# A scheduler's account of the port that GpSimd and VectorE share, GpSimd's traced durations, and a settings string found anew, in a kernel of two attention and two FFN layers

## The chip, the cores and the metric

The kernel runs on one core of a Trainium2 chip. A core has five engines, each with an instruction stream of its own: TensorE (PE in the profile; PEld is its weight load), ScalarE (ACT), VectorE (DVE), GpSimd (POOL) and SyncE (SP), which here issues the DMAs. The metric is the device time of one launch in microseconds (us), as the median of several runs.

## The reference

`x` has 2048 rows of 512, all in bf16. Attention A and FFN B are applied twice with the same weights, each behind a layer normalization and added to `x`:

```python
def _A_ref(x, wqkv, wo):            # D = 512, H = 32 heads of Dh = 16
    qkv = (x @ wqkv).reshape(B, S, 3, H, Dh).transpose(2, 0, 3, 1, 4)
    q, k, v = qkv[0], qkv[1], qkv[2]
    p = _softmax(jnp.einsum("bhqd,bhkd->bhqk", q, k) * Dh ** -0.5)
    o = jnp.einsum("bhqk,bhkd->bhqd", p, v)
    return o.transpose(0, 2, 1, 3).reshape(B, S, D) @ wo
def _B_ref(x, w1, b1, w2, b2):      # F = 1376
    h = _gelu(jnp.einsum("bsd,df->bsf", _layernorm(x), w1) + b1)
    return jnp.einsum("bsf,fd->bsd", h, w2) + b2
x = A_x
x = x + _A_ref(_layernorm(x), A_wqkv, A_wo)
x = x + _B_ref(_layernorm(x), B_w1, B_b1, B_w2, B_b2)
x = x + _A_ref(_layernorm(x), A_wqkv, A_wo)
x = x + _B_ref(_layernorm(x), B_w1, B_b1, B_w2, B_b2)
```

The heavy part is the softmax: 32 heads x 2048 x 2048 scores in each of two layers, 268 million exponentials in all.

## The kernel before, in words

**Layers and segments.** The four steps are called layers 0 to 3 in the code: `L` is 1 for the first attention and FFN, 3 for the second. Heads go in eight groups of four (`hg`), queries in units of 512 (`units`, `qc`); the last unit of layer 3 is cut into 256, 128 and 128 queries. One unit and one head group make a segment. The first unit of either layer is cut over the keys too: part 0 takes the key tiles that are ready early, part 1 the others, and the two are merged with running sums. In layer 1, part 0 is the first 4 of the 16 key tiles and part 1 the other 12; in layer 3 it is 12 and 4. All eight head groups go through part 0 before part 1 begins (`build_segments`).

**One score tile.** A tile is 128 keys by 512 queries of one head. PE computes it into one PSUM bank (L1536, four heads beside each other in the array). Then one of two engines takes the exponential. ACT does it for groups of two or three banks at once (L1521, output `PT`). DVE does it for one bank at a time: L1628 reads the bank and writes the scores, scaled beforehand, as 16-bit integers, whose bits are those of an approximate bf16 exponential; shift copies then add constants to these bits (L1659 of 1024 elements, then L1667 of 2048), so that four terms stand for one tile. Two batches that are due together are joined to one copy (L1614 and L1615, twice the size). The code calls these D tiles. PE multiplies the results into the accumulator (L1741: `PT` and `dp` against `V` for plain values, and against `vs`, scaled copies of V, for the shifted terms). When a segment is through, `job_segend` transposes the accumulator on DVE (L1771), merges the parts on POOL (L1784, L1792 to L1795), divides (L1797, L1801, L1807) and passes it to the output projection (L1821).

**What must come before a part's scores.** The scores carry a bound on each query's largest score, made from norms of q and k. When a part begins, `job_scl` works out the bound on the keys: a maximum `nm` on DVE (L1223), its transpose on PE (L1225), a maximum on DVE, a square root on POOL (L1228, a power), a product on DVE (`krhs`), a small matmul on PE (L1231), and `scl` on DVE (L1232). Only then can `job_qt` write the scaled queries `QT` (L1262; on DVE for five segments, on POOL for the others), and only then can the part's scores go out. Other work of POOL: `vs` (L1287), the normalizations' application in layers' middles (`ln_apply`, L951), their reciprocal roots (`ln_group`, the power in L942), bounds on the queries (L1095 to L1099), squares (L1057), a memset (L859).

**What sets the order.** `Sched` simulates the five engines in Python and writes out every engine's instructions in the order in which its simulation issued them; on the chip each engine follows its list, and semaphores hold an instruction until what it reads is there. Each task has a priority and instructions with planned durations in microseconds. `best` picks for an engine the task of lowest priority number among those whose inputs are ready (`task_ready`, L382); scores have 0.0, products with V 1.0, D tiles' shift copies 0.15 to 2.5, `job_scl` and `job_qt` some 0.3 to 0.5. `post_prio` (L1828) gives the priority of what follows a unit's attention: 0.95 for the last two units of layer 1 and those of layer 3 from `LATE3` on, else 2.2. Of that, the FFN's additions of the bias (L1911) run at it minus 0.7, and the normalization and the projections q, k and v of the next layer (L1016, `job_lnqkv`) at it minus 0.8. `d_solo` and `take_d` give a tile to DVE when its planned work is short.

**The settings string.** `Hint.ORDER` has one base-36 digit for every four groups of exponentials (`STEP`). A digit picks one of 12 `MODES`: each changes one threshold of the scheduler, as how short DVE's work must be to give it a tile (`D_IDLE`), how full a turn of products must be (`PV_LEAST`), how late scores may be before other PE work is held (`HOLD_LATE`). So the string reshuffles the whole order without changing what is computed.

**The port.** The plan knows that a POOL instruction slows DVE's fast copies. `self.hits` (L79) keeps POOL's last four instructions with their planned times and a penalty (`lat` of a POOL instruction, 0.09 to 0.38). A DVE instruction marked "fast" (the shift copies and some others) that overlaps one in the plan is lengthened by that penalty; POOL is never delayed by DVE in the plan (L141 to L144).

**Fillers and tail.** Behind the schedule, `refill` lays the plan once more and puts matmuls on zeros (`zw`, L1425, L1427, L1429) into PE's gaps, sized in the plan. `job_tail` orders the end: the last exponentials, a table load for Gelu (L1998), Gelu on ACT (L1934, L1935) over what the FFN's first matrix product (L1882) and the additions L1911 have left for the unit ahead (in `h`), its second product (L1943), transposes behind the last normalization (L2053), and the last unit's own FFN (L1882, L2004).

## Time and profile before

| | us |
|---|---|
| median of 3 runs | 1540.3 (1538.06, 1540.3, 1541.64) |
| span of the profiled execution | 1535.9 |
| profiled execution's own time around that span | not shown |
| ACT busy | 1502.5 |
| PE busy, fillers included | 1486.8 |
| DVE busy | 1442.2 |
| POOL busy | 343.0 |
| PE's zero matmuls, L1429, L1427 and L1425 | 147.1, 119.5 and 87.4 |

A row of the profile names a line, engine, operation and its tiles, then the count, the busy time and the mean of one in ns, and last the idle time of the engine just ahead of these instructions with what ended most of it. A timeline's row begins with the start and the duration in us; neighbouring instructions of one form are drawn together (x10), and square brackets at the end hold the idle time before. A row of the chain that ended last has the start, the time that it adds, engine, tile and line. PE's matmuls overlap, so that its share isn't a utilization; idle time of an engine that isn't the bound costs nothing.

### The profile page before, as it was taken

The page shows a single profiled execution, that of the slowest core. Times are in us where ns is not written, and L with a number is a line of the kernel's source. Part 1 is how long each engine was busy: PE and PEld are TensorE (multiplying, and loading weights), DVE is VectorE, ACT ScalarE, POOL GpSimd, SP SyncE. Part 2 cuts the span into 40 slices and gives each one's busy share as a digit, 9 for nine tenths or more (in the row PEclk, how much of TensorE's full clock was granted, in tenths as well). Part 3 has the DMA queues.
Part 4 walks back from the last instruction along what each step waited for, and adds up shares of the span by engine and source line. Part 5 has one row for each costly group of instructions (what it writes and reads, how often), then busy time and mean ns, then how long its engine had stood idle before and what let it go on. Part 6 is the DMA issues. An engine that isn't in the chain of part 4 may idle for free.

```text
span 1535.9 us, 41170 instructions
## 1 busy us (share of the span) xinstructions
PE 1486.8 (97%) x17654; PEld 491.3 (32%) x17654; DVE 1442.2 (94%) x2661; ACT 1502.5 (98%) x1346; POOL 343.0 (22%) x570
## 2 busy tenths in 40 slices
PE   9999999999999999999999999999999999999998
PEld 3222222222222222222322332222222222344555
DVE  8799999999999999999999899999999989998786
ACT  8999999999999999999999999999999999999897
POOL 3576321102120022202322138220002000020110
PEclk9999999999999999999999999999999999999999
DMA  6663102213312123214842332210011001120221
GB/s 163 120 154 91 32 22 34 51 35 68 82 48 63 37 64 84 56 35 100 138 69 64 60 87 63 53 30 18 22 36 35 14 27 32 36 49 18 73 67 30
DMA packets 212487, 90.55 MB, mean 59 GB/s; under 512 B 182251, under 2 KB 207184, under 8 KB 212304
## 3 DMA queue, kind: packets, MB, share of 16 engines
q1 hardware_dynamic: 212304, 87.92, 25.6%
q8 instruction: 138, 2.26, 0.6%
q14 instruction: 45, 0.37, 0.1%
HBM read 36.81 MB, written 19.48 MB: 37 GB/s over the span
## 4 chain that ended last, share of the span: by engine, by line
ACT 44%; PE 27%; DVE 24%; issue 3%; POOL 2%; DMA 0%; DVEq 0%; POOLq 0%
ACT PT L1521 41%; DVE dp L1628 10%; PE ps L1536 9%; PE ps L1741 8%; PE ps L1943 3%; DVE dp L1667 3%; PE ps L1882 2%; PE ps L1016 2%; ACT h L1934 2%; DVE dp L1615 2%; DVE dp L1659 1%; PE ps L1425 1%; DVE accT L1771 1%; DVE st L933 1%; DVE dp L1614 1%
## 5 line engine op out<-in xcount | busy, mean ns | idle before, releaser
L1521 ACT ACTIVATE PT<-ps 128x1536 bf16<-128x1536 f32 (+1 forms) x1256 | 1422.0, 1309 | 20.6 <-PE ps L1536 18.8
L1628 DVE TENSOR_SCALAR dp<-ps 128x512 uint16<-128x512 f32 x979 | 648.8, 679 | 33.7 <-PE ps L1536 30.4
L1536 PE MATMUL ps<-QT,KT 32*128 32x512 bf16 (+2 forms) x5120 | 602.6, 340 | 23.9 <-ACT PT L1521 7.5
L1741 PE MATMUL ps<-PT,V 128*17 128x512 bf16 (+2 forms) x3899 | 491.1, 338 | 0.6 <-issue 0.5
L1741 PE MATMUL ps<-dp,vs 128*17 128x512 bf16 (+2 forms) x3663 | 460.8, 339 | 2.7 <-issue 1.8
L1536 PEld LDWEIGHTS ps<-QT,KT 32*128 32x128 bf16 x5120 | 174.1, 91 | 543.6 <-ACT PT L1521 297.6
L1262 POOL TENSOR_SCALAR QT<-qraw,scl,qbias 128x512 bf16<-128x512 bf16 (+2 forms) x91 | 75.2, 827 | 762.8 <-PE ps L1536 754.3
L1741 PE MATMUL ps<-dp,V 128*17 128x512 bf16 (+2 forms) x1221 | 232.3, 340 | 1.6 <-DVE accT L1771 1.2
L1667 DVE TENSOR_SCALAR dp<-dp 128x2048 uint16<-128x2048 uint16 x310 | 214.3, 694 | 4.9 <-PE ps L1741 1.8
L1741 PEld LDWEIGHTS ps<-dp,vs 128*17 128x17 bf16 x3663 | 124.1, 89 | 114.1 <-issue 84.8
L1741 PEld LDWEIGHTS ps<-PT,V 128*17 128x17 bf16 x3899 | 126.9, 89 | 94.2 <-issue 75.1
L1429 PE MATMUL ps<-zw 128*32 128x448 bf16 (+23 forms) x1514 | 147.1, 322 | 0.1
L1659 DVE TENSOR_SCALAR dp<-dp 128x1024 uint16<-128x1024 uint16 (+1 forms) x298 | 126.1, 426 | 2.6
L1427 PE MATMUL ps<-zw 32*128 32x444 bf16 (+7 forms) x386 | 119.5, 332 | 0.0
L1615 DVE TENSOR_SCALAR dp<-dp 128x4096 uint16<-128x4096 uint16 x91 | 111.0, 1225 | 0.6 <-PE ps L1741 0.4
L1882 PE MATMUL ps<-yT,wf 128*128 128x512 bf16 (+5 forms) x440 | 102.7, 340 | 2.1 <-issue 1.0
L1016 PE MATMUL ps<-wqkv,xnT 128*128 128x512 bf16 x336 | 91.7, 382 | 4.1 <-DVE h L1029 1.1
L1425 PE MATMUL ps<-zw 128*128 128x448 bf16 (+14 forms) x347 | 87.4, 338 | 4.4 <-DVE onec L809 2.1
L1287 POOL TENSOR_SCALAR vs<-V 128x340 bf16<-128x340 bf16 (+2 forms) x72 | 64.3, 894 | 23.0 <-PE ps L1741 16.2
L1741 PEld LDWEIGHTS ps<-dp,V 128*17 128x17 bf16 x1221 | 58.2, 89 | 34.6 <-issue 19.4
L1614 DVE TENSOR_SCALAR dp<-dp 128x2048 uint16<-128x2048 uint16 x97 | 67.8, 700 | 0.0
L1771 DVE STREAM_TRANSPOSE accT<-ps 128x512 f32<-128x512 f32 (+2 forms) x96 | 59.2, 617 | 5.3 <-PE ps L1741 5.0
(201 smaller groups left out, 1053.4 us busy)
## 6 DMA issues: line engine op xcount, KB each, us to landing
vs<-vs_scr SPq DMA_DIRECT2D x64, 255.0 KB, 2.8
wf<-in_B_w_dram SPq DMA_DIRECT2D x90, 128.0 KB, 2.5
q_scr<-qk SPq DMA_DIRECT2D x20, 256.0 KB, 2.0
k_scr<-qk SPq DMA_DIRECT2D x12, 256.0 KB, 2.1
out_dram<-xres SPq DMA_DIRECT2D x16, 128.0 KB, 1.7
vs_scr<-vs SPq DMA_DIRECT2D x8, 255.0 KB, 3.3
xres<-in_A_x_dram SPq DMA_DIRECT2D x7, 256.0 KB, 5.3
v_scr<-vst SPq DMA_DIRECT2D x12, 136.0 KB, 1.7
```

Of the source, the lines that this page charges most:

```text
L1016: yield Task("pe", prio if c0 == 0 else min(prio, HINT.LIN2), [I(lambda e, c=c: e.matmul(self.ps[:, b, :], lhsT=xnT[:, c, :], rhs=self.wqk ...
L1425: fn = lambda e: e.matmul(self.ps[:, b, 0:w], lhsT=self.zw[:, 0:128], rhs=self.zw[:, 0:w], start=st, stop=st, skip_group_check=True)
L1427: fn = lambda e: e.matmul(self.ps[:, b, 0:w], lhsT=self.zw[32 * p:32 * p + 32, 0:128], rhs=self.zw[32 * p:32 * p + 32, 0:w], start=st, sto ...
L1429: fn = lambda e: e.matmul(self.ps[32 * p:32 * p + 32, b, 0:w], lhsT=self.zw[:, 0:32], rhs=self.zw[:, 0:w], start=st, stop=st, skip_group_c ...
L1521: S_.submit(Task("act", 1e-5 * gi, [I(lambda e, pt=pt, n=n, b0=b0: e.activation(out=self.PT[:, pt:pt + n, :], in_=self.ps[:, b0:b0 + n, :] ...
L1536: return [I(lambda e, kb=kb, i=i: e.matmul(self.ps[:, b, i * W:(i + 1) * W], lhsT=self.KT[32 * hp:32 * hp + 32, hg, kb * 128:(kb + 1) * 12 ...
L1615: return lambda e: e.tensor_scalar(out=self.both(x[1], y[1]), in0=self.both(x[0], y[0]), scalar1=float(SHIFT[2]), scalar2=None, op0=ALU.add)
L1628: self.S_.submit(Task("dve", 0.0, [I(lambda e: e.tensor_scalar(out=self.dpu(u)[:, w * 512:(w + 1) * 512], in0=self.ps[:, b, :], scalar1=BI ...
L1659: t = Task("dve", prio(), [I(lambda e: e.tensor_scalar(out=self.dpu(u + 1)[:, 0:N], in0=self.dpu(u)[:, 0:N], scalar1=float(SHIFT[1]), scal ...
L1667: t = Task("dve", prio(), [I(lambda e: e.tensor_scalar(out=self.dpp(v)[:, :, 0:N], in0=self.dpp(u)[:, :, 0:N], scalar1=float(SHIFT[2]), sc ...
L1741: ops.append((nth[j, sh] + 0.1 * i, I(lambda e, hp=hp, v=v, ap=ap[:, i * W:(i + 1) * W], first=first and i == 0, W=W: e.matmul(self.ps[32 ...
L1882: yield Task("pe", self.soft(pr if c0 == 0 else min(pr, HINT.LIN2)) if y0 == 0 else pr, [I(lambda e, c=c: e.matmul(self.ps[0:M, b, 0:W], l ...
```

## The change

The account of the port is written anew. Two fields hold until when DVE's last fast copy and POOL's last instruction hold the port. In the plan a POOL instruction now starts its body (behind a head of 0.2 us) only when DVE's fast copy is through, and a fast copy starts its body (behind 0.137 us) only when a POOL body that began before it is through. POOL instructions marked "brief" wait but don't hold the port. `task_ready` counts the port as an input of fast instructions. POOL's planned durations are set to those of traces, the penalties go, and more instructions of DVE carry the mark "fast". `post_prio` is 0.7 for layer 1's last unit. `ORDER` is another string. Lines of the changed kernel stand 20 higher than before: L1225 is L1245 there, L1536 is L1556, and so on.

```diff
+POOL_HEAD = 0.2
+DVE_HEAD = 0.137
...
-        self.hits = []
+        self.dve_port = (0.0, None)
+        self.pool_port = (0.0, 0.0)
...
             if eng == "pool":
-                self.hits = self.hits[-3:] + [(op.t0, op.t0 + dur, lat or 0.0)]
+                if lat == "after" and self.dve_port[1] is not None:
+                    order = self.dve_port[1]
+                    op.t0 = max(op.t0, order.t1 + LATENCY["pool"])
+                body = max(op.t0 + POOL_HEAD, self.dve_port[0])
+                dur = body + max(0.0, dur - POOL_HEAD) - op.t0
+                if lat != "brief":
+                    self.pool_port = (body, op.t0 + dur)
                 lat = None
             elif lat == "fast":
-                dur += sum(h for t0, t1, h in self.hits if t0 < op.t0 + dur and op.t0 < t1)
+                body = op.t0 + DVE_HEAD
+                if self.pool_port[0] <= body:
+                    body = max(body, self.pool_port[1])
+                dur = body + dur - DVE_HEAD - op.t0
+                self.dve_port = (op.t0 + dur, op)
                 lat = None
...
+            if lat == "fast":
+                r = max(r, P.pool_port[1] - DVE_HEAD)
+            elif lat == "after":
+                r = max(r, P.dve_port[0] + LATENCY["pool"])
         return r
...
-    ORDER = '617843148821304205503107024723209000040207043042340397211914350542770442973009430070000450240024504940493349800001430000505010133104559a211a2540320233040
+    ORDER = '570045030800534070003002303031403011030303420031020034192500022b801b50250500300400000803023509000452700079002734800534200030954433a3559a70034a55a507024090
...
     def ln_apply(self, tt, slot, i, dst, dres, prio, eng="dve"):
...
-                                         [("x", tt), ("nmr", slot), ("rs", slot)], [dres], 0.92, (), 0.09)])
+                                         [("x", tt), ("nmr", slot), ("rs", slot)], [dres], 0.77)])
...
     def job_qt(self, sg, s):
...
-0.16 + 0.24 * W / 512 if eng == "dve" else 0.43 + 0.52 * W / 512, (), "fast" if eng == "dve" else 0.09)])
+0.16 + 0.24 * W / 512 if eng == "dve" else 0.34 + 0.43 * W / 512, (), "fast" if eng == "dve" else None)])
...
     def post_prio(self, L, qc):
-        return 0.95 if L == 1 and qc >= self.NC - 2 or L == 3 and qc >= LATE3 else 2.2
+        return 0.7 if L == 1 and qc == self.NC - 1 else 0.95 if L == 1 and qc >= self.NC - 2 or L == 3 and qc >= LATE3 else 2.2
```

The durations not shown: `vs` 0.27 + 0.17 for each key tile to 0.21 + 0.17; the segment's merges 0.70 to 0.62 and 0.75 to 0.73; the powers 0.45 to 0.42 (plus 0.153 a column) and, in `job_scl`, 0.55 to 0.60, both "brief"; the bounds' small products 0.26 to 0.38 before, 0.22 to 0.33 now, "brief".

The change moves instructions in nearly every row of the order. Three places follow. The first is PE where layer 3 goes from part 0 to part 1, as it was: L1225 transposes `nm`, L1231 multiplies `krhs`, L1536 are scores, L1741 products with V.

```order
L1536 MATMUL ps<-QT,KT 128x512 x3
L1427 MATMUL ps<-zw 128x444
L1741 MATMUL ps<-PT,V 17x512
L1741 MATMUL ps<-dp,vs 17x512
L1741 MATMUL ps<-PT,V 17x512 x2
L1741 MATMUL ps<-dp,vs 17x512 x3
L1429 MATMUL ps<-zw 32x444
L1429 MATMUL ps<-zw 32x366 x4
L1225 MATMUL ps<-ident,nm 32x128
L1741 MATMUL ps<-dp,vs 17x512
L1741 MATMUL ps<-PT,V 17x512 x3
L1741 MATMUL ps<-dp,V 17x512
```

And as it is now:

```order
L1245 MATMUL ps<-ident,nm 32x128
L1556 MATMUL ps<-QT,KT 128x512 x2
L1447 MATMUL ps<-zw 128x444
L1556 MATMUL ps<-QT,KT 128x512
L1447 MATMUL ps<-zw 128x444
L1761 MATMUL ps<-PT,V 17x512
L1761 MATMUL ps<-dp,vs 17x512
L1761 MATMUL ps<-PT,V 17x512 x3
...
L1761 MATMUL ps<-dp,vs 17x512 x2
L1556 MATMUL ps<-QT,KT 128x512 x2
L1251 MATMUL ps<-krhs,sel 128x8
```

Before, the last scores of part 0 stand ahead of L1225, and the next scores come 14 rows behind L1231; now five tiles of scores stand between L1245 and L1251. The second place is PE where layer 1 goes from part 0 to part 1, as it was:

```order
L1225 MATMUL ps<-ident,nm 32x128
L1536 MATMUL ps<-QT,KT 128x512 x2
L1427 MATMUL ps<-zw 128x444
L1741 MATMUL ps<-PT,V 17x512 x4
L1429 MATMUL ps<-zw 32x448 x8
L1429 MATMUL ps<-zw 32x226 x4
L1536 MATMUL ps<-QT,KT 128x512 x3
L1741 MATMUL ps<-PT,V 17x512 x3
L1429 MATMUL ps<-zw 32x444
L1429 MATMUL ps<-zw 32x200 x4
L1231 MATMUL ps<-krhs,sel 128x8
```

And as it is now:

```order
L1556 MATMUL ps<-QT,KT 128x512 x3
L1761 MATMUL ps<-PT,V 17x512 x3
L1449 MATMUL ps<-zw 32x444
...
L1245 MATMUL ps<-ident,nm 32x128
L1761 MATMUL ps<-PT,V 17x512
...
L1251 MATMUL ps<-krhs,sel 128x8
L1445 MATMUL ps<-zw 128x448 x3
L1445 MATMUL ps<-zw 128x398
L1556 MATMUL ps<-QT,KT 128x512
```

Before, five tiles of scores stand between the two small matmuls; now the last scores of part 0 stand ahead of both, with products and fillers behind them. The third place is DVE's end: L1771 transposes the accumulator, L1797 and L1801 divide, L1803 transposes the result for the projection, L1911 adds the FFN's bias. As it was:

```order
L1659 TENSOR_SCALAR dp<-dp 128x1024
L1667 TENSOR_SCALAR dp<-dp 128x2048
L1911 TENSOR_SCALAR h<-ps,b1c 96x128
L1771 STREAM_TRANSPOSE accT<-ps 128x128
L1797 RECIPROCAL rv<-accT 128x4
L1801 TENSOR_TENSOR obl<-accT,rv 128x4x16
L1803 STREAM_TRANSPOSE dp<-obl 128x128
```

And as it is now:

```order
L1823 STREAM_TRANSPOSE dp<-obl 128x128
L1931 TENSOR_SCALAR h<-ps,b1c 128x128
L1791 STREAM_TRANSPOSE accT<-ps 128x128
L1931 TENSOR_SCALAR h<-ps,b1c 128x128
L1817 RECIPROCAL rv<-accT 128x4
L1931 TENSOR_SCALAR h<-ps,b1c 128x128
L1821 TENSOR_TENSOR obl<-accT,rv 128x4x16
L1931 TENSOR_SCALAR h<-ps,b1c 128x128 x4
L1823 STREAM_TRANSPOSE dp<-obl 128x128
L1931 TENSOR_SCALAR h<-ps,b1c 96x128
```

Before, the last addition L1911 stands ahead of the last two heads' ends; now eight additions stand behind the last but one L1823 (which was L1803).

55 lines of the change are left out of this document (29 added, 26 removed).

## The prediction

> **What bounds the kernel now.** I read the page first, then the groups by shape, the waits, the timeline at the longest waits, and the chain that ended last.
>
> The page, its first row and the group of the attention exponentials:
>
> ```profile
> PE 1486.8 (97%) x17654; PEld 491.3 (32%) x17654; DVE 1442.2 (94%) x2661; ACT 1502.5 (98%) x1346; POOL 343.0 (22%) x570
> L1521 ACT ACTIVATE PT<-ps 128x1536 bf16<-128x1536 f32 (+1 forms) x1256 | 1422.0, 1309 | 20.6 <-PE ps L1536 18.8
> ```
>
> ScalarE (ACT) is busy 98% of 1535.9 us, and VectorE (DVE) 94%. PE's 97% holds filler matmuls on zeros and says little. ACT stands still for 33.4 us in all, 20.6 of them ahead of its exponentials. GpSimd (POOL) is busy for 22%: a change in its timing acts only through DVE, which meets it at a port, or through a chain that POOL is a link of. So the kernel's time is ACT's work, plus ACT's waits, plus a short start and tail. I count the change in those terms.
>
> The group of exponentials by shape:
>
> ```profile
> L1521 ACT ACTIVATE PT<-ps 128x1536 bf16<-128x1536 f32 x605 | 924.6, 1528 | 14.6 <-PE ps L1536 13.2
> L1521 ACT ACTIVATE PT<-ps 128x1024 bf16<-128x1024 f32 x651 | 712.5, 1105 | 5.9 <-PE ps L1536 5.7
> ```
>
> One more bank of 512 columns costs 1528 - 1105 = 423 ns. The 605 x 3 + 651 x 2 = 3117 banks take 1318.5 us of the 1422.0, and the remaining 103.5 us over 1256 instructions is 82 ns for each instruction.
>
> DVE's part of the softmax, by shape:
>
> ```profile
> L1628 DVE TENSOR_SCALAR dp<-ps 128x512 uint16<-128x512 f32 x979 | 648.8, 679 | 33.7 <-PE ps L1536 30.4
> L1667 DVE TENSOR_SCALAR dp<-dp 128x2048 uint16<-128x2048 uint16 x305 | 212.2, 699 | 4.9 <-PE ps L1741 1.8
> L1659 DVE TENSOR_SCALAR dp<-dp 128x1024 uint16<-128x1024 uint16 x293 | 124.7, 429 | 2.6
> L1615 DVE TENSOR_SCALAR dp<-dp 128x4096 uint16<-128x4096 uint16 x91 | 111.0, 1225 | 0.6 <-PE ps L1741 0.4
> L1614 DVE TENSOR_SCALAR dp<-dp 128x2048 uint16<-128x2048 uint16 x97 | 67.8, 700 | 0.0
> ```
>
> The last four are the shift copies, which meet POOL. What a meeting costs shows in the timelines of POOL and of DVE around 1432 us:
>
> ```profile
> 1432.14 1.53 POOL L859 MEMSET dp<- 128x512 bf16 x2 [7.69 <-PE ps L1741]
> 1433.13 0.82 DVE L1659 TENSOR_SCALAR dp<-dp 128x1024 uint16<-128x1024 uint16 x1
> 1437.06 0.42 DVE L1659 TENSOR_SCALAR dp<-dp 128x1024 uint16<-128x1024 uint16 x1
> 1437.52 0.69 DVE L1667 TENSOR_SCALAR dp<-dp 128x2048 uint16<-128x2048 uint16 x1
> ```
>
> Beside POOL's memsets the copy of 1024 takes 0.82 us, alone 0.42. On the mean the port costs little: against an undisturbed 0.42 and 0.68 (the 0.69 above is its display to 10 ns), 293 x 0.009 + 305 x 0.019 + 97 x 0.020 = 10.4 us of DVE time in the three largest groups. That is the stock from which a better account of the port can draw; it's not on ACT's clock until DVE is late with a bank or a P tile.
>
> **The change, part by part.** *The account alone* runs nowhere on the chip. It and the new ORDER string decide which instruction stands where; the sum is over the places where that shows.
>
> *Work moved between ACT and DVE.* Counting rows, ACT issues 604 exponentials of three banks and 655 of two: 3122 banks in 1259 instructions, 5 and 3 more. That is 5 x 0.423 + 3 x 0.082 = **+2.4 us** on the engine that bounds. DVE gets 974 loads for 979 (-3.4 us), 9 fewer joined copies at L1614 (-6.3) and 6 fewer at L1615 (-7.4), against 21 more single copies at L1659 and 15 more at L1667, 11 of each short: at 0.28 and 0.42 apiece (what the page's totals, next, leave for the five short ones of before) that is +7.4 and +7.4. DVE is 2.3 us lighter, which doesn't lie on the path: ACT doesn't wait for DVE's sum.
>
> ```profile
> L1667 DVE TENSOR_SCALAR dp<-dp 128x2048 uint16<-128x2048 uint16 x310 | 214.3, 694 | 4.9 <-PE ps L1741 1.8
> L1659 DVE TENSOR_SCALAR dp<-dp 128x1024 uint16<-128x1024 uint16 (+1 forms) x298 | 126.1, 426 | 2.6
> ```
>
> *The change of part in layer 3.* ACT's longest wait of the steady state and the chain behind it (timelines of ACT, PE, POOL):
>
> ```profile
> 920.45 11.40 ACT L1521 ACTIVATE PT<-ps 128x1024 bf16<-128x1024 f32 x10 [2.47 <-PE ps L1536]
> 915.78 0.39 PE L1536 MATMUL ps<-QT,KT 32*128 32x512 bf16 x3
> 916.84 0.23 PE L1225 MATMUL ps<-ident,nm 128*32 128x128 bf16 x1
> 918.58 0.17 PE L1231 MATMUL ps<-krhs,sel 32*128 32x8 bf16 x1
> 919.20 1.52 POOL L1262 TENSOR_SCALAR QT<-qraw,scl,qbias 128x512 bf16<-128x512 bf16 x2 [0.22 <-DVE scl L1232]
> 920.02 0.39 PE L1536 MATMUL ps<-QT,KT 32*128 32x512 bf16 x4
> ```
>
> The last scores of part 0 go out at 915.78, ACT is through with them at 917.98, and the first scores of part 1 need the key bound (L1225, L1231) and QT: 3.18 us from L1225 to them. In the changed order five score tiles stand behind the transpose of the bound, two of them just ahead of L1231's successor; ACT gets 5 x 0.423 + 2 x 0.082 = 2.3 us more to do inside the chain. The 2.47 us shrink to some 0.2: **-2.3 us**. Bounds: -2.47 if all goes, 0 if the chain itself gets later by as much, since its start hangs on the last tiles of layer 1.
>
> *The change of part in layer 1* goes the other way. Before (chain that ended last, and ACT's timeline):
>
> ```profile
> 75.92 1.40 PE ps L1016 x6
> 82.33 0.17 PE ps L1231
> 83.50 0.44 PE ps L1536 x3
> 83.93 7.80 ACT L1521 ACTIVATE PT<-ps 128x1024 bf16<-128x1024 f32 x7 [0.27 <-PE ps L1536]
> ```
>
> Here the chain costs ACT 0.27 us, since 13 score tiles stand behind the last projections (L1016), 5 of them behind L1225. In the new order all 128 tiles of part 0 stand ahead of the transpose and nothing between it and the first scores of part 1: the picture of 916 us above, with QT on DVE, which isn't slower. There ACT waited 2.47, so here it should wait about 2.2 more than its 0.27, unless the start is quicker: ACT also waits elsewhere in its first 60 us, the longest for 1.37 us:
>
> ```profile
> 36.64 20.73 ACT L1521 ACTIVATE PT<-ps 128x1536 bf16<-128x1536 f32 x18 [1.37 <-PE ps L1536]
> ```
>
> What is saved there is lost in the wait behind it, and the net is the arrival of the chain. I take **+1.5 us**, between -0.3 (all of the 0.27 gone) and +3.3 (the whole 3.18 chain bare and its last link).
>
> *The tail.* The chain that ended last, and four rows of DVE:
>
> ```profile
> 1521.25 1.28 ACT L1998
> 1522.74 1.17 ACT h L1934
> 1524.30 2.33 PE ps L1943 x10
> 1526.63 0.24 PE ps L2053 x4
> 1516.97 0.34 DVE L1911 TENSOR_SCALAR h<-ps,b1c 128x128 bf16<-128x128 f32 x1
> 1517.23 0.41 DVE L1659 TENSOR_SCALAR dp<-dp 128x1024 uint16<-128x1024 uint16 x1
> 1518.29 0.34 DVE L1911 TENSOR_SCALAR h<-ps,b1c 96x128 bf16<-96x128 f32 x1
> 1522.55 0.31 DVE L1803 STREAM_TRANSPOSE dp<-obl 128x128 bf16<-128x128 bf16 x1
> ```
>
> Before, the last FFN1 result of the unit ahead (L1911) is out at 1518.6, so that Gelu starts as soon as its table is in. In the new order 28 of its matmuls stand behind the last PV, and eight of its additions behind the last transpose but one (L1803), six of them between the last L1771 and the last L1803. At 0.26 us from start to start (1517.23 - 1516.97) five hold the transpose back by 1.3 us (the sixth falls into the gaps between dependent instructions), and Gelu, behind the eighth, starts near 1524.5 and not at 1522.7. Two of the ten L1943 now stand behind L2053, which gives back 2 x 0.23. **+1.3 us**, between 0 and +1.9. The cover that hid this work before were the last exponentials.
>
> *The port.* ACT's 18.8 us behind scores were 48 waits. Without the 2.47, 1.37 and the 2.13 below, 12.8 us are left in 45 waits of 0.28 us: this is jitter, of which the lock may be one cause. If the planner now lays other work under a held port, a part goes. Upper bound of the gain: 10.4 us of DVE, if each were ACT's; lower: nothing, or a loss of the same kind as the scatter moves, which I set at 2. I take a quarter of the 12.8: **-3.2 us**. For what POOL holds, the row:
>
> ```profile
> 699.10 1.04 POOL L942 TENSOR_TENSOR rs<-rs,cneg 128x4 f32<-128x4 f32 x1
> 699.22 0.68 DVE L1614 TENSOR_SCALAR dp<-dp 128x2048 uint16<-128x2048 uint16 x1
> ```
>
> The copy that begins inside the power runs in its undisturbed 0.68 us, as the new mark "brief" has it. The Trainium skill, in "SBUF — State Buffer", section "Who interferes with whom", says that whichever engine issues first has the shared pair for the whole instruction and the other fully blocks. By that the copy would have ended only after 1.04 - 0.12 + 0.68 us, and the new marks would leave out waits of up to 0.9 us at each of the 19 powers, 17 us of DVE at most; the trace doesn't agree for these small operands, and the sum goes by the row.
>
> *The stall at 1437 us.*
>
> ```profile
> 1439.20 0.22 PE L1741 MATMUL ps<-dp,vs 128*17 128x128 bf16 x1 [1.84 <-issue]
> 1439.91 2.37 ACT L1521 ACTIVATE PT<-ps 128x1536 bf16<-128x1536 f32 x2 [2.13 <-PE ps L1536]
> ```
>
> PE stands for 1.84 us behind nothing that the profile shows, in the stage of narrow tiles, and ACT pays 2.13. No rule of the scheduler knows of it. It may go or come again elsewhere: 0, between -2.1 and +2.1.
>
> **Sum:** 2.4 - 2.3 + 1.5 + 1.3 - 3.2 + 0 = -0.3 us on the profiled 1535.9. What lies around the span isn't shown for that execution; the median of the runs, 1540.3, stands 4.4 above it, and I keep that: **1540.0 us, no change**. Its own range, with the unknown terms each some way to their bounds, is 1537 to 1543. A measurement can tell 0.2% here, 3.1 us, since the runs shown lie 3.6 apart.
>
> **The rivals.**
>
> *The port was the cause of most small waits.* Then the account takes out two thirds of the 12.8 us, and the stall at 1437, which follows the memsets that held DVE, goes with them: -0.3 - 5.3 - 2.1 gives 1532.6. For it: the 0.82 against 0.42, and that POOL's late copies stand in both long chains. Against it: only 10.4 us of DVE, and five tiles less for DVE in the new order, which doesn't look like an engine with time to spare.
>
> *Layer 1's last projections crowd the scores.* post_prio is 0.7 for the last unit of layer 1, so that its normalization and layer 3's projections run at -0.1, ahead of the scores' 0.0. In the new order most projections stand four in a row. The row of the first such stage:
>
> ```profile
> 102.44 1.02 PE L1016 MATMUL ps<-wqkv,xnT 128*128 128x512 bf16 x4
> ```
>
> Four take 1.0 us; with the scores (0.39) and eight PVs (0.6, x8 of 0.39 in two turns) PE needs 2.0 us where ACT's two-bank group covers 1.1. If each of 12 such blocks costs ACT 0.4 us, 4.8 us come on: 1544.8. It decides from the block on at which both score groups are spent, 0.3 us each. Against it: the order puts no two blocks together, and the other group of scores lies between.
>
> *The change doesn't do what it says*: a string found on the planner's clock orders 1535 us of work on five engines, and its gain there is lost in the scatter between plan and chip. Then it is any time between 1533 and 1547, 1540 in the middle.
>
> **How the numbers follow.** The forecast 0.40 (faster 0.09, same 0.27, slower 0.04), the port 0.28 (faster 0.26, same 0.02), the crowding 0.20 (same 0.03, slower 0.17), no bearing 0.12 (faster 0.04, same 0.03, slower 0.05). So faster 0.39, same 0.35, slower 0.26. The range runs from 1532 to 1546: it takes in the port's centre and the crowding's.
>
> **What would show it.** In the changed profile: exponentials x604 and x655, ACT busy near 1505; at the change of part in layer 3 a wait of ACT under 0.5 us where 2.47 stood; a wait near 2 us close to 84 us; the Gelu behind the last exponential some 1.8 us after its table; the mean of L1667 and of L1659 nearer 680 and 420. If ACT's idle time ahead of the exponentials falls under 14 us, the port had more to it than I think; if it rises over 24, the new order crowds PE. The forecast is wrong if the small waits move by more than 3 us either way, whatever the four places do.

## The result: 0.5% slower

The changed kernel takes 1548.4 us (median of 5 runs, 1542.3 to 1551.4) against 1538.4 for the kernel before in the same measurement (5 runs, 1538.1 to 1541.6): ratio 1.0053, 95% interval [1.0033, 1.0073]. The forecast was no change, 1540.0, with a range up to 1546; the time lies outside it.

The profiled execution took 1551.41 us, and its span is 1549.6, so that 1.8 us lie around the span. It is the slowest of the five. The five times go with their mean granted TensorE clock, if not in strict order: 1542.3 at 1.000, 1548.5 at 0.998, 1548.4 at 0.997, 1547.6 at 0.996, 1551.4 at 0.994. The kernel before has 0.999 in its profile. Part of the loss is therefore in stretches at a lower clock, which are shown below. The execution at 1.000 lies 3.9 us above 1538.4, so that by an estimate from this one execution some 6 of the median's 10.0 us go with the clock. The profile, of the slowest execution, shows more of that than the median holds.

First the page of the changed kernel, and its groups by shape:

```profile
PE 1478.8 (95%) x17718; PEld 496.5 (32%) x17848; DVE 1438.9 (93%) x2677; ACT 1507.2 (97%) x1349; POOL 340.3 (22%) x570
L1541 ACT ACTIVATE PT<-ps 128x1536 bf16<-128x1536 f32 x604 | 909.3, 1506 | 20.3 <-PE ps L1556 17.1
L1541 ACT ACTIVATE PT<-ps 128x1024 bf16<-128x1024 f32 x655 | 702.3, 1083 | 7.7 <-PE ps L1556 7.1
L1648 DVE TENSOR_SCALAR dp<-ps 128x512 uint16<-128x512 f32 x974 | 646.0, 681 | 45.3 <-PE ps L1556 40.8
L1687 DVE TENSOR_SCALAR dp<-dp 128x2048 uint16<-128x2048 uint16 x309 | 215.1, 699 | 6.7 <-PE ps L1761 3.4 <-PE ps L1556 0.4
L1679 DVE TENSOR_SCALAR dp<-dp 128x1024 uint16<-128x1024 uint16 x303 | 128.9, 428 | 2.5
```

The span grew by 13.7 us: ACT is busy for 4.7 more, and idle for 42.4 where it was 33.4, 9.0 more. The idle time ahead of the exponentials went from 20.6 to 28.0. DVE's idle time ahead of its score loads went from 33.7 to 45.3. The two largest groups of shift copies have kept their means: 699 for 699 and 428 for 429 ns. Whatever the account of the port changed in the plan, these copies meet POOL on the chip as before.

**Where the 13.7 us arose.** The score tiles are the same 4096 in both kernels, so one can ask at what time the k-th of them had gone through its exponential on ACT or its load on DVE. The difference of the two curves, worked out from the ends of all rows of L1541 and L1648 (L1521 and L1628 before), after minus before:

| tile | before, us | after, us | difference |
|---|---|---|---|
| 384 | 178.1 | 176.6 | -1.4 |
| 1920 | 728.0 | 727.7 | -0.3 |
| 2112 | 794.1 | 801.6 | +7.5 |
| 2176 | 816.2 | 829.2 | +13.0 |
| 3712 | 1366.9 | 1380.7 | +13.8 |
| 3776 | 1389.6 | 1407.1 | +17.4 |
| 3904 | 1444.9 | 1458.6 | +13.6 |
| last | 1521.2 | 1532.7 | +11.5 |
| end of span | 1535.9 | 1549.6 | +13.7 |

At tile 1920 the two are level. Between 1920 and 2176, where layer 1 gives way to layer 3, 13.3 us go. Another 3.6 go near 1384 us; some 4 come back near 1440, where the kernel before has its own stall; the tail costs 2.2.

**The change from layer 1 to layer 3, first half (tiles 1984 to 2112).** The windows of the two profiles between these tiles (start and end, length, then busy time and count of PE, PEld, DVE, ACT, POOL, the granted clock, the DMA share and GB/s), and the groups of tiles inside them. First before:

```profile
750.60:794.10 43.50, 42.32 (x472) 13.40 (x470) 43.31 (x74) 43.05 (x39) 14.67 (x17) 1.00 0.79 116
L1521 ACT ACTIVATE PT<-ps 128x1536 bf16<-128x1536 f32 x19 | 29.4, 1550 | 0.5 <-PE ps L1536 0.5
L1521 ACT ACTIVATE PT<-ps 128x1024 bf16<-128x1024 f32 x20 | 22.6, 1128 | 0.0
L1628 DVE TENSOR_SCALAR dp<-ps 128x512 uint16<-128x512 f32 x33 | 21.6, 676 | 0.0
```

Then after:

```profile
751.10:801.60 50.50, 48.30 (x487) 14.93 (x490) 41.19 (x76) 48.09 (x44) 16.78 (x27) 1.00 0.89 150
L1541 ACT ACTIVATE PT<-ps 128x1536 bf16<-128x1536 f32 x22 | 32.5, 1477 | 2.4 <-PE ps L1556 2.3
L1541 ACT ACTIVATE PT<-ps 128x1024 bf16<-128x1024 f32 x22 | 23.2, 1054 | 0.0
L1648 DVE TENSOR_SCALAR dp<-ps 128x512 uint16<-128x512 f32 x23 | 15.3, 679 | 4.4 <-PE ps L1556 4.2
```

DVE was idle for 0.2 us in 43.5 and is now idle for 9.3 in 50.5. It loads 23 tiles where it loaded 33, and ACT takes the ten as well: about 105 banks for about 95 (the groups cut at the windows' edges hold 110 and 97). Ten banks are 4.2 us of ACT at 0.42 each, and ACT's own idle time grew from 0.45 to 2.41. That is 6.2 of the 7.0 us. The remainder is busy time of ACT; that neighbouring exponentials overlap less when waits come between them would explain it, and isn't measured here by itself. The timeline of DVE shows the hole:

```profile
772.39 1.22 DVE L1635 TENSOR_SCALAR dp<-dp 128x4096 uint16<-128x4096 uint16 x1
778.00 0.72 DVE L1791 STREAM_TRANSPOSE accT<-ps 128x512 f32<-128x512 f32 x1 [4.39 <-PE ps L1761]
783.15 3.31 DVE L1648 TENSOR_SCALAR dp<-ps 128x512 uint16<-128x512 f32 x5 [3.68 <-PE ps L1556]
```

From 773.6 to 783.15 DVE has the end of one segment to do and no score tile. PE isn't short of time, as it puts zeros into the same stretch:

```profile
775.81 1.50 PE L1445 MATMUL ps<-zw 128*128 128x448 bf16 x7
```

The order gives DVE no scores here. In it the processing of q, k and v for layer 3's key tiles 8 to 11 stands later: at tile 1984, DVE had 252.9 us of its other work (all but loads and shift copies) behind it, before 262.0. Layer 3's first key load stands at score tile 2015 in place of 1960, its first V load at 2046 in place of 1992.

**The second half (tiles 2112 to 2176).** ACT's longest wait here, and what stands ahead of it, in four timelines (POOL, DVE, PE, ACT):

```profile
802.84 2.75 POOL L1307 TENSOR_SCALAR vs<-V 128x204 bf16<-128x204 bf16 x3 [7.53 <-DMA vs_scr<-vs]
805.53 0.40 POOL L1804 COPY dp<-accT 128x256 f32<-128x256 f32 x1
806.44 1.03 POOL L962 TENSOR_TENSOR rs<-rs,cneg 128x4 f32<-128x4 f32 x1
807.51 1.06 DVE L973 TENSOR_SCALAR xn<-xres,mv,rs 128x512 bf16<-128x512 bf16 x3 [3.09 <-POOL rs L962]
809.23 0.38 PE L1556 MATMUL ps<-QT,KT 32*128 32x512 bf16 x1 [2.65 <-DVE dp L1648]
811.20 2.52 ACT L1541 ACTIVATE PT<-ps 128x1536 bf16<-128x1536 f32 x2 [2.80 <-PE ps L1556]
815.13 1.45 ACT L1541 ACTIVATE PT<-ps 128x1536 bf16<-128x1536 f32 x1 [1.41 <-PE ps L1556]
```

POOL stands for 7.53 us behind a transfer, then writes `vs`, copies a segment's accumulator, and only then takes up the power that a normalization needs (L962). DVE waits for that power with score loads behind it in its list, PE waits for a bank that DVE hasn't emptied, and ACT for PE. Before, the same power stood behind nothing that was late:

```profile
789.99 2.28 POOL L1287 TENSOR_SCALAR vs<-V 128x204 bf16<-128x204 bf16 x3 [1.28 <-PE ps L1741]
800.79 1.04 POOL L942 TENSOR_TENSOR rs<-rs,cneg 128x4 f32<-128x4 f32 x1
```

The rows of SP's queue show what that transfer stands behind. The transposes and loads for layer 3 have come 54 tiles later and meet those of the last segments of layer 1:

```profile
781.58 6.24 SPq L1836 DMA_TRANSPOSE dp<-ob  x4
787.87 5.34 SPq L1323 DMA_DIRECT2D V<-v_scr  x5
796.77 2.42 SPq L1314 DMA_DIRECT2D vs_scr<-vs  x3
```

Of the 5.5 us lost here, 2.80 are the first wait. The later two, 2.30 together, come with a lower clock, in the windows of the changed kernel:

```profile
805.00:810.00 5.00, 2.27 (x19) 0.68 (x18) 2.49 (x6) 3.40 (x4) 2.74 (x7) 1.00 0.25 58
810.00:815.00 5.00, 5.00 (x27) 1.02 (x25) 4.32 (x7) 2.48 (x2) 0.00 (x0) 0.55 0.63 80
815.00:820.00 5.00, 4.84 (x54) 1.36 (x51) 3.58 (x7) 3.97 (x4) 0.77 (x1) 0.76 0.01 2
...
1385.00:1390.00 5.00, 5.00 (x64) 1.82 (x58) 2.97 (x6) 3.73 (x4) 0.00 (x0) 0.50 0.51 115
1390.00:1395.00 5.00, 4.84 (x73) 2.26 (x66) 3.47 (x6) 2.75 (x3) 0.14 (x1) 0.58 0.00 0
```

TensorE runs at half its clock from 810.5 for 6.8 us and from 1384.0 for 10.2 us. The kernel before has one such stretch, 3.4 us long at 1440.9, behind the stall that the prediction quotes.

**The other three places.** ACT where layer 1 goes to part 1, where layer 3 does, and at the end; then three rows of DVE at the end:

```profile
83.57 25.04 ACT L1541 ACTIVATE PT<-ps 128x1024 bf16<-128x1024 f32 x22 [3.26 <-PE ps L1556]
933.13 9.15 ACT L1541 ACTIVATE PT<-ps 128x1536 bf16<-128x1536 f32 x8 [0.86 <-PE ps L1556]
1532.73 1.28 ACT L2018 ACT_TABLE_LOAD   x1
1536.80 1.27 ACT L1954 ACTIVATE h<-h 128x1280 bf16<-128x1280 bf16 x1 [2.57 <-DVE h L1931]
...
1533.61 0.35 DVE L1931 TENSOR_SCALAR h<-ps,b1c 128x128 bf16<-128x128 f32 x1 [2.69 <-PE ps L1902]
1535.19 1.13 DVE L1931 TENSOR_SCALAR h<-ps,b1c 128x128 bf16<-128x128 f32 x4
1536.23 0.30 DVE L1823 STREAM_TRANSPOSE dp<-obl 128x128 bf16<-128x128 bf16 x1
```

### The profile page after: what moved, and what is told of

It is laid out like the page before. It is cut to its first block, busy times and chain, and to the rows that moved or that the text cites. A ratio compares the mean times of both kernels' runs of the same rounds, so it can differ in the third digit from the quotient of the medians.

```text
span 1549.6 us, 41482 instructions
## 1 busy us (share of the span) xinstructions
PE 1478.8 (95%) x17718; PEld 496.5 (32%) x17848; DVE 1438.9 (93%) x2677; ACT 1507.2 (97%) x1349; POOL 340.3 (22%) x570
## 4 chain that ended last, share of the span: by engine, by line
ACT 37%; PE 29%; DVE 27%; issue 3%; SPq 2%; POOL 1%; DMA 1%; DVEq 0%; POOLq 0%
ACT PT L1541 34%; DVE dp L1648 11%; PE ps L1556 10%; PE ps L1761 9%; DVE dp L1687 3%; PE ps L1963 3%; PE ps L1902 2%; DVE dp L1635 2%; ACT h L1954 2%; PE ps L1036 2%; DVE dp L1679 2%; DVE accT L1791 1%; PE ps L1445 1%; PE ps L1449 1%; DVE st L953 1%
## 5 line engine op out<-in xcount | busy, mean ns | idle before, releaser
L1541 ACT ACTIVATE PT<-ps 128x1536 bf16<-128x1536 f32 (+1 forms) x1259 | 1426.8, 1285 | 28.0 <-PE ps L1556 24.2
L1648 DVE TENSOR_SCALAR dp<-ps 128x512 uint16<-128x512 f32 x974 | 646.0, 681 | 45.3 <-PE ps L1556 40.8
L1556 PE MATMUL ps<-QT,KT 32*128 32x512 bf16 (+2 forms) x5120 | 603.2, 341 | 25.1 <-DVE dp L1648 10.6
L1761 PE MATMUL ps<-dp,vs 128*17 128x512 bf16 (+2 forms) x3660 | 466.6, 340 | 1.6 <-issue 0.6
L1556 PEld LDWEIGHTS ps<-QT,KT 32*128 32x128 bf16 x5120 | 174.5, 91 | 541.4 <-ACT PT L1541 266.4
L1687 DVE TENSOR_SCALAR dp<-dp 128x2048 uint16<-128x2048 uint16 (+1 forms) x325 | 222.7, 688 | 6.9 <-PE ps L1761 3.4
L1449 PE MATMUL ps<-zw 128*32 128x448 bf16 (+20 forms) x1716 | 180.0, 323 | 0.8 <-DVE dp L1648 0.7
L1679 DVE TENSOR_SCALAR dp<-dp 128x1024 uint16<-128x1024 uint16 (+1 forms) x319 | 133.5, 421 | 2.6
L1447 PE MATMUL ps<-zw 32*128 32x444 bf16 (+3 forms) x403 | 123.9, 332 | 0.0
L1635 DVE TENSOR_SCALAR dp<-dp 128x4096 uint16<-128x4096 uint16 x85 | 105.0, 1236 | 0.2
L1902 PE MATMUL ps<-yT,wf 128*128 128x512 bf16 (+5 forms) x400 | 93.5, 336 | 8.0 <-issue 5.1
L1036 PE MATMUL ps<-wqkv,xnT 128*128 128x512 bf16 x303 | 84.0, 382 | 6.7 <-issue 3.3
L1445 PE MATMUL ps<-zw 128*128 128x448 bf16 (+19 forms) x325 | 79.7, 340 | 4.9 <-DVE onec L829 2.1
L1307 POOL TENSOR_SCALAR vs<-V 128x340 bf16<-128x340 bf16 (+2 forms) x72 | 64.6, 898 | 33.4 <-PE ps L1761 12.0
L1449 PEld LDWEIGHTS ps<-zw 128*32 128x32 bf16 x1716 | 62.9, 95 | 24.7 <-DVE dp L1648 4.1
```

The costliest lines, as they stand in the source:

```text
L1036: yield Task("pe", prio if c0 == 0 else min(prio, HINT.LIN2), [I(lambda e, c=c: e.matmul(self.ps[:, b, :], lhsT=xnT[:, c, :], rhs=self.wqk ...
L1445: fn = lambda e: e.matmul(self.ps[:, b, 0:w], lhsT=self.zw[:, 0:128], rhs=self.zw[:, 0:w], start=st, stop=st, skip_group_check=True)
L1447: fn = lambda e: e.matmul(self.ps[:, b, 0:w], lhsT=self.zw[32 * p:32 * p + 32, 0:128], rhs=self.zw[32 * p:32 * p + 32, 0:w], start=st, sto ...
L1449: fn = lambda e: e.matmul(self.ps[32 * p:32 * p + 32, b, 0:w], lhsT=self.zw[:, 0:32], rhs=self.zw[:, 0:w], start=st, stop=st, skip_group_c ...
L1541: S_.submit(Task("act", 1e-5 * gi, [I(lambda e, pt=pt, n=n, b0=b0: e.activation(out=self.PT[:, pt:pt + n, :], in_=self.ps[:, b0:b0 + n, :] ...
L1556: return [I(lambda e, kb=kb, i=i: e.matmul(self.ps[:, b, i * W:(i + 1) * W], lhsT=self.KT[32 * hp:32 * hp + 32, hg, kb * 128:(kb + 1) * 12 ...
```

## The experiments

Ten kernels ran. All compare with the kernel before on the same chip. Four of them ran once each, and their differences are against the 1536.5 us which that kernel took beside them. Four lines of thought were tested: that POOL's order makes the stall at 806 us; that too few zeros between PE's work let the clock fall; that the string fits only the account and the priority with which it was found; and that DVE does lie on the path, which the prediction denied.

### POOL's power ahead of `vs`

The changed kernel with the instructions of one normalization's root (L961, L962, L965, L966) ahead of the three `vs` and the two copies of L1804, and the store of `vs` (L1314) behind three transposes that it stood ahead of; nothing else moves.

```diff
-        self.refill()
+        self.refill(), relay(self)
...
+    late = [i for i in range(k - 70, k) if ops[i].eng == "pool" and ops[i].writes[0][0] in ("vs", "OT", "den")]
+    store = [i for i in range(k - 40, k) if ops[i].eng == "sp" and ops[i].writes[0][0] == "vsscr"]
...
+    ops[k - 70:yt] = keep(k - 70, end) + [ops[i] for i in late] + keep(end, yt) + [ops[i] for i in store]
```

> The changed kernel; in POOL's order alone the normalization's root (L961, L962, L965, L966) of layer 1's last unit stands ahead of the three vs copies (L1307) and the merge (L1804) that stood before it, and the store of that vs goes out behind three of the transposes L1892; every other instruction stands where it stood. Theory 1 (few places and the clock): POOL came to the root late because the vs ahead of it waited 7.53 us for a store's landing; DVE stood 3.09 us behind the root, PE 2.65 us behind DVE, ACT 2.80 us behind PE, and the window with PE idle was followed by 6.8 us at half clock, which cost ACT another 2.3. All of it goes: DVE's wait ahead of L973 under 0.5 us, no half clock near 810 us, the profiled span some 5 us shorter than 1549.6 and the median near 1544 (the dip near 1384 us stays). Theory 2 (the new account slows the whole plan, spread over all of it): ACT finds its 5 us of waits elsewhere and the median stays within 1 us of 1548.4.

Measured: 1540.7 us (10 runs, 1539.7 to 1542.3) against 1536.7 (22 runs); ratio 1.0026 [1.0017, 1.0035]. The changed kernel itself is at 1.0053. The timelines of POOL and of ACT in this kernel:

```profile
801.40 1.03 POOL L962 TENSOR_TENSOR rs<-rs,cneg 128x4 f32<-128x4 f32 x1
803.09 2.28 POOL L1307 TENSOR_SCALAR vs<-V 128x204 bf16<-128x204 bf16 x3
```

```profile
774.78 60.85 ACT L1541 ACTIVATE PT<-ps 128x1536 bf16<-128x1536 f32 x53 [1.37 <-PE ps L1556]
```

The power comes 5 us earlier, and ACT runs from 774.78 to 835.6 without a wait. The clock is 1.000, also at 1384 us. On the curve of tiles it stands 6.0 us behind the kernel before at tile 2112, as the changed kernel does nearly (7.5), but 6.0 still at 2176 where that has 13.0, and 0.9 at the last exponential. So the order of POOL's list made the second half of the loss at the layer change, and the half-clock stretch there with it: the loss against the kernel before fell from 10.0 to 4.0 us, and nine of the ten executions ran at a clock of 1.000, the tenth at 0.999. The first half stays. Why the stretch at 1384 went too, this run doesn't tell: the same instructions stand there, some 7 us earlier. That is also why this run came out below its expectation, which counted on the stall alone.

### More zeros

In the changed kernel, in the kernel of the last experiment, and in the kernel before, the share of PE's time that the fillers aim at is raised; 538 to 574 more matmuls on zeros come in, the other instructions keep their order.

```diff
-FILL_U = 0.55
+FILL_U = 0.7
```

> The changed kernel with FILL_U 0.7 for 0.55: more zero matmuls in PE's planned gaps (2982 for 2444), all other instructions of all engines in the same order. Theory 1: the stretch from 1380.6 us, in which PE worked at about a third of its full rate, is filled, and the 10.2 us at half clock behind it go, worth 3.5 us in the executions that had it; the one near 810 us stays, since its idle time was not planned and gets no fillers. Median 1545, mean granted clock 0.998 or more. If fillers hold up real work, PE's in-order queue makes ACT wait more, 1550 or more. Theory 2: no change, 1548.

> Both edits together on the changed kernel. Theory 1: no stretch at half clock is left but at the very end, mean granted clock 0.999 or more, all executions within 2 us of each other near 1540 to 1541, still 2 to 3 us above the kernel before: the tail's 2.2 us and the weaker stretch from 750 to 800 us are left. Theory 2: 1546 or more.

> The kernel before with FILL_U 0.7 for 0.55 and nothing else. Theory 1 (a stretch of low PE activity halves the clock, and this is what spreads the executions from 1538.1 to 1541.6): the 3.4 us at half clock behind the stall at 1438 us need not go, since the stall isn't planned, but marginal stretches do: the executions lie within 1.5 us of each other and the median is 0 to 2 us below the kernel before. If fillers cost as much as they save: within 0.1% either way. Theory 2 says nothing here.

Measured: the changed kernel with them 1547.2 us (6 runs, 1542.8 to 1551.5), ratio 1.0069 [1.0051, 1.0088]; with the power moved too 1545.3 (5 runs), 1.0051 [1.0035, 1.0068]; the kernel before with them 1539.1 (11 runs), 1.0014 [1.0004, 1.0024]. More zeros gain nothing in any of the three. They cost about 2 us in the kernel before, and about 4 where the power is moved. None of the three came out as expected, which was 1545 for the first, 1540 to 1541 with all executions within 2 us for the second (1540.7 to 1546.0 came), and 0 to 2 us below the kernel before, with executions within 1.5 us, for the third (1536.0 to 1542.6 came). The windows of the first, in the profile of one execution, show where the clock fell:

```profile
270.00:275.00 5.00, 3.09 (x18) 0.52 (x18) 3.39 (x5) 2.67 (x3) 0.00 (x0) 0.67 0.19 39
275.00:280.00 5.00, 5.00 (x41) 1.04 (x39) 2.60 (x5) 3.16 (x4) 0.00 (x0) 0.65 0.09 26
...
1385.00:1390.00 5.00, 5.00 (x115) 2.59 (x115) 5.00 (x10) 5.00 (x6) 0.00 (x0) 1.00 0.72 113
```

At 1385 the clock is full now, and 3.0 us are won there against the changed kernel (tiles 3712 to 3776 on the curve). But another stretch has come up at 271.7 us, which costs 4.3 (tiles 640 to 704). A third difference is at the layer change. POOL's order is the changed kernel's, with the power behind `vs` and the copies (808.44 us), yet this execution loses 1.6 us there (tiles 2112 to 2176) and not 5.5. The expectation had the half clock near 810 us stay, and it isn't there. DVE's and ACT's rows:

```profile
809.51 1.06 DVE L973 TENSOR_SCALAR xn<-xres,mv,rs 128x512 bf16<-128x512 bf16 x3 [1.52 <-POOL rs L962]
812.98 6.95 ACT L1541 ACTIVATE PT<-ps 128x1536 bf16<-128x1536 f32 x6 [1.01 <-PE ps L1556]
```

DVE waits for half as long, and ACT for 1.01 us where it was 2.80. So the same lists cost from 1.6 to 5.5 us at this place, by how far POOL is behind DVE in an execution and whether the clock then falls. That more zeros cure the fall of the clock is refuted by the three times.

### One part of the change at a time

Four kernels, each run once: the new account and durations with the old string and priority; the old account with the new string and priority; the kernel before with the new priority alone; the changed kernel with the old priority. The last two are this line, forward and back:

```diff
-        return 0.95 if L == 1 and qc >= self.NC - 2 or L == 3 and qc >= LATE3 else 2.2
+        return 0.7 if L == 1 and qc == self.NC - 1 else 0.95 if L == 1 and qc >= self.NC - 2 or L == 3 and qc >= LATE3 else 2.2
```

> The new account, marks and POOL durations with the old settings string and the old priority. Theory 3 (a string only fits the account under which it was found: the first place where the new costs turn a decision shifts what every later digit meets): far slower than either kernel, 1570 to 1595 us, the loss spread over all of the span at 2 to 3%. Theory 2 (the new costs make the plan slower by themselves, and the new string wins back a part): 1545 to 1560. If the account were what gains and the string what loses: under 1538.

> The old account and durations with the new settings string and the new priority. Theory 3: 1570 to 1595 us as well, so that neither half of the change can be called the cause by itself. Theory 2: close to the changed kernel without its stretches at half clock, 1540 to 1550, since the order would come from the string.

> The kernel before with post_prio 0.7 for layer 1's last unit and nothing else; no instruction moves until that unit's attention is through, at about tile 2100 of the 4096 score tiles. Theory 3: equal to the kernel before up to there (within 0.5 us by tile 2048), then a loss that grows to 10 to 18 us over the second half, since the old digits meet other decisions. If the priority itself crowds the scores: the loss is there at once, 4 to 5 us between tiles 2100 and 2500.

> The changed kernel with the old priority for layer 1's last unit. The order is the same up to about tile 2100, so the loss against the kernel before between tiles 1984 and 2112 (7 us in the changed kernel) stays, within 1 us: it isn't the priority's. Behind it theory 3 has 10 to 20 us more than the changed kernel's plain order, 1555 to 1565 us in all; whether POOL's root is late and DVE stands behind it is open.

Measured: 1580.7, 1588.7, 1554.7 and 1559.0 us. Each part alone, and the whole with one part undone, is slower than both kernels, and than the one before by 18 to 52 us. For the first two the difference on the curve of tiles grows from the start (12.1 and 14.7 us at tile 960, 24 at 1920), where nothing particular stands; no one place is responsible. All four came out where, or within a microsecond of where, their expectations had a string that fits only the account and the priority with which it was found. By these single runs that fit is worth 44 to 52 us for the account and 11 to 18 for the priority, and what the account alone is worth can't be read from a kernel with any string that wasn't found with it. That also bars the reading that the new account by itself is bad.

Two things can still be read. With the priority undone the order is the changed kernel's up to tile 1920 (-1.5) and behind by 5.7 at tile 2112: the first half of the loss at the layer change isn't the new priority's. The rival in which that priority crowds PE isn't settled. The span is 7.6 us longer without it, but that order is another one from the layer change on, with a string that wasn't found for it. At the place itself, tiles 2112 to 2176, the run without the priority loses 0.9 us and not 5.5: POOL's `vs` waits there too (5.45 us), but the power comes at 802.53 and DVE stands only 0.90 behind it.

### DVE with more, and with less to do

The kernel before with 20 of DVE's 979 loads done twice, evenly spread (the second writes the same values again); and the kernel before with 19 of the 305 second shift copies (L1667) left out, so that the products read what stood in those buffers. All lists keep their order.

```diff
+        P.op(*op.spec)
+        if op.eng == "dve" and op.spec[5] == 0.682:
+            n += 1
+            if n % 49 == 25:
+                P.op(*op.spec)
```

> The kernel before, with 20 of DVE's 979 loads of a score bank done twice, spread evenly (every 49th): the same result is written again, all other instructions stand as they stood. 20 x 0.6 us (the pitch of neighbouring loads) = 12 us more work for DVE, on PE and ACT nothing. The prediction's step says that DVE doesn't lie on the path, since ACT doesn't wait for DVE's sum: then the span grows by 0 to 2 us, and DVE's idle time of 93.7 us falls by about 12. Against it stands that DVE's and ACT's tiles leave by one list of PE and feed one list of products, so that where DVE has no idle time of its own (the stretches of the attention away from the part changes) each 0.6 us comes out at PE and then at ACT: then the span grows by most of the 12, 8 to 13 us, ACT's busy time stays, and DVE's idle time stays near 94.

> The kernel before with 19 of DVE's 305 second shift copies of 2048 elements left out (every 15th), so that the products read what stood in those buffers; all other instructions stand as they stood. 19 x 0.6 us = 11.4 us less work for DVE. If DVE's time is the kernel's time in both directions, the span falls by 6 to 11 us. If DVE off the path is right, by 0 to 1. A third way: lists fix which engine takes which tile, so that a DVE that is early only waits for its next scores; then more DVE work costs its full time (see the other run) while less gains nothing, 0 to 2 us, and DVE's idle time rises by about 11 us.

Measured: with more 1549.5 us (4 runs) against 1536.2 (13 runs), ratio 1.0088 [1.0071, 1.0104]; with less 1536.1 (10 runs), ratio 0.9992 [0.9980, 1.0004]. The pages, with more and then with less:

```profile
PE 1491.1 (96%) x17654; PEld 490.6 (32%) x17654; DVE 1454.4 (94%) x2681; ACT 1506.3 (97%) x1346; POOL 346.6 (22%) x570
L1521 ACT ACTIVATE PT<-ps 128x1536 bf16<-128x1536 f32 (+1 forms) x1256 | 1425.6, 1286 | 26.7 <-PE ps L1536 23.7
```

```profile
PE 1486.0 (97%) x17654; PEld 490.2 (32%) x17654; DVE 1432.8 (93%) x2642; ACT 1502.0 (98%) x1346; POOL 343.1 (22%) x570
L1521 ACT ACTIVATE PT<-ps 128x1536 bf16<-128x1536 f32 (+1 forms) x1256 | 1421.4, 1312 | 18.9 <-PE ps L1536 17.1
```

12.2 us more of DVE cost 13.4 us between the medians (10.9 to 16.0 by the ratio's interval), and 9.7 on the profiled span of 1545.6. There DVE's idle time is 91.2 us, where it was 93.7: the work found no gap to go into. ACT's busy time is 3.8 us longer at the same instructions, since neighbouring exponentials overlap less when waits come between them, and its idle time 5.9; the expectation had ACT's busy time unchanged. A load done twice also holds its PSUM bank longer, and this run doesn't part that from DVE's own time. In the other direction 9.4 us less of DVE's work gain nothing that can be told from zero, and 7.7 of them appear as new idle time of DVE (101.4 on a span of 1534.2). The two together are as the third way in the second expectation had it.

Set beside the others, each value from the page of its profile, this reads:

| kernel | span | DVE busy | DVE idle | ACT busy | ACT idle |
|---|---|---|---|---|---|
| before | 1535.9 | 1442.2 | 93.7 | 1502.5 | 33.4 |
| power ahead of `vs` | 1539.0 | 1439.5 | 99.5 | 1506.5 | 32.5 |
| after | 1549.6 | 1438.9 | 110.7 | 1507.2 | 42.4 |
| priority alone | 1552.9 | 1442.2 | 110.7 | 1508.0 | 44.9 |
| priority undone | 1557.2 | 1434.1 | 123.1 | 1513.1 | 44.1 |
| account alone | 1578.9 | 1426.7 | 152.2 | 1524.8 | 54.1 |
| string alone | 1586.9 | 1435.8 | 151.1 | 1520.0 | 66.9 |

Among these the span rises with the idle time of DVE as clearly as with that of ACT. In part this is arithmetic, since idle time is the span less a busy time that differs by no more than 16 us (DVE) and 22 us (ACT) over the table; it shows where time was lost and not which engine lost it. A tile that DVE doesn't take, ACT must: its banks are 3117 before and 3145 with the account alone, which is 11.8 of that run's 43 us at 0.423 each.

## Why the prediction was wrong

**"DVE is 2.3 us lighter, which doesn't lie on the path: ACT doesn't wait for DVE's sum."** This step failed as a rule, and with it the statement ahead of the prediction that idle time of an engine that isn't the bound costs nothing. It holds in one direction: less work for DVE in the same lists gained nothing, and DVE is in fact 3.3 us lighter here (1438.9 for 1442.2). In the other direction more work cost its full length. What counts isn't DVE's sum but where DVE is late. Its wait of 3.09 us behind POOL's power went on to PE (2.65) and to ACT (2.80). And the two engines divide one stock of tiles, so that a stretch in which DVE has no tile is paid by ACT with 0.42 us a bank, which isn't seen in ACT's waits. Counting ACT's idle time as the whole stock from which a loss or gain could come, I missed that.

**The places of the sum.** "The sum is over the places where that shows": this is the step that cost most. I took the two changes of part, the tail and the small waits. The 13.3 us between tiles 1920 and 2176 are in a place that the sum doesn't contain, the change from layer 1 to layer 3, since ACT's waits of the kernel before show nothing there (0.5 us between 750.6 and 794.1). I put that place at nothing without a reason. The experiment with the power ahead of `vs` takes the part between tiles 2112 and 2176 from 5.5 us to nothing. Some of the 13.3 is a term that the sum does contain: DVE had taken 458 tiles for 454 by tile 1984 and 481 for 487 by tile 2112, and ends five behind, so that the net five banks of the next paragraph (2.4 us) lie in it. The order as it was changed would have shown layer 3's first key load 55 score tiles later, and `vs` in POOL's list ahead of a power.

**Work moved, +2.4:** right. 604 and 655 exponentials as counted; ACT's busy time grew by 4.7, of which the other 2.3 fit lost overlap, a cost that the prediction had no term for.

**Layer 3's change of part, -2.3:** the mechanism was right, the size off: the wait is 0.86 us and not 0.2, 1.6 less than the 2.47 before, and the curve of tiles falls by 1 to 2 us across it, depending on which tiles are compared.

**Layer 1's change of part, +1.5:** the wait came as foreseen, 3.26 us, but part 1 starts at 83.57 where it started at 83.93: all of it had been won beforehand. The term is -0.4, at the lower bound that the prediction gave it (-0.3).

**The port, -3.2:** nothing came of it. The means of the two largest groups of copies are unchanged to a nanosecond, and the idle time ahead of the exponentials rose. The rival that makes the port the cause of most small waits, which counted on a relief of the port, isn't borne out; since the port wasn't relieved, what it costs stays untested. What the new account finds in the plan isn't disproved; this string didn't turn it into time.

**The tail, +1.3:** the mechanism was right, the size off: it is +2.2 from the last exponential to the end of the span. The additions L1931 stand ahead of the last transpose and hold it back, as foreseen, and Gelu starts 4.07 us behind the start of its table load (1.40 before). I had counted their pitch alone. But the first of them waits 2.69 us for the matmuls L1902, which now stand behind the last products, and goes out 0.9 us after the last exponential's end, so that the last transpose comes at 1536.23, 3.5 us behind that end, where it came at 1.3.

**The stall at 1437, 0 with ±2.1:** the question wasn't that stall but its kind. A stretch with little work on the array can be followed by a stretch at half clock. The changed kernel has two of these in its profile, 17 us long together. I had the half-clock stretch of the kernel before in the quoted rows' neighbourhood and didn't look at the clock there.

**The offset of 4.4** was a misreading of the runs' scatter: between time and span lie 1.7 to 1.9 us in the profiled executions for which both are known. By that the sum would have gone to 1537.4.

**Rivals and what would show it.** The time lies above the upper end (1547) of the rival that had the gain lost in scatter, which came nearest in kind. The note that idle time over 24 us ahead of the exponentials would mean a crowded PE gave the sign and not the cause: 28.0 us came, but PE put zeros into the hole at 775 us and stood for 2.65 at 809. Whether the earlier projections had a part in that wait is open, as the run without the priority shows.

**What stays open.** The first half of the loss at the layer change, 6 to 7.5 us, is read from the traces and the order, so its cause is argued and not shown; no run undid it, since the order there depends on all digits of the string before it. Why the order with the power ahead of `vs` keeps the full clock at 1384 us isn't shown either. That SP's queue is what makes `vs` late rests on the rows of that queue. What the new account of the port would gain in itself is open too.

## What to carry to other kernels

Where two engines share one stock of work by fixed lists, idle time of the lesser one can be as dear as that of the bound, where it comes of lateness: compare both engines' idle time stage by stage, and the count of pieces each takes, ahead of any wait. In the lists tried here lateness cost its full length and earliness gained nothing, so a forecast should have more on the slow side than its terms' bounds say. A table of settings that was searched for with one cost model is part of that model: test neither without the other, and when the order is new, look first at the place where most queues meet (here the change of layers), for a short instruction that stands behind a late transfer.

## What was not expected of the hardware

**Half clock without an idle PE.** All stretches at half clock that these profiles show inside the attention are 3.4, 6.8 or 10.2 us long, multiples of 3.41. I worked out the share of the array's rate that the matmuls used in each 3.41 us on the same grid (columns streamed against those of full-rate zeros, with a quarter for matmuls of at most 32 rows or 32 columns). How a matmul across an edge is counted moves these shares by some 0.02. The window ahead of a half-clock stretch had 0.26 and 0.34 in the changed kernel, 0.30 in the one before, 0.36 in the changed one with more zeros, 0.35 in the one with more DVE work. In these profiles, outside such stretches and away from the ends, one window at 0.37 and all at 0.39 or above weren't followed by one. In the kernel with the power ahead of `vs`, which keeps its clock, the lowest is 0.42. But a low share isn't always followed by a stretch: in the changed kernel with the old priority the window from 1394.8 us has 0.31, with PE idle for 1.77 of its 3.41 us, and the clock stayed full. So the share tells where the clock may fall, and no threshold is shown. At 1384 us PE hadn't been idle:

```profile
1379.80:1383.20 3.40, 3.09 (x57) 1.08 (x51) 3.37 (x6) 3.40 (x4) 3.18 (x5) 1.00 0.16 33
1383.20:1386.60 3.40, 3.39 (x37) 1.30 (x31) 2.72 (x8) 3.05 (x3) 1.52 (x3) 0.61 0.57 133
```

It was busy for 3.09 of 3.40 us, with narrow matmuls that overlap each other, and then lost the clock. The Trainium skill, in "TensorE: Matmul & The Clock Gate", section "HAM oscillation — how this bites in real kernels", gives the rule as no idle gap of PE over about 3.4 us. The stretches' lengths agree with a window of 3.4 us. No gap in the changed kernel's attention reached that (the longest, 2.65 us, is the one at 809), and the clock fell twice, so the trace doesn't agree with a rule by gaps alone.

**The port asks more of POOL than of DVE.** A small product of 0.20 us stretches beside DVE's joined copies:

```profile
1376.64 1.14 POOL L961 TENSOR_SCALAR rs<-mv 128x4 f32<-128x4 f32 x1 [6.72 <-DVE mv L954]
1376.49 2.36 DVE L1635 TENSOR_SCALAR dp<-dp 128x4096 uint16<-128x4096 uint16 x2
```

It takes 1.14 us beside copies that take their usual 1.22 apiece, while the copy that the prediction quotes kept its 0.68 us inside a power of 1.04. Here the port delayed a small instruction of POOL, and with it what waits for that; two rows show it, and no run tested it.
